# V of the second and third batch by row loads into the odd key spans, instead of by casts and moves, in a fused window attention and shrink MLP

## Chip, cores and metric

One core of one Trainium2 chip. The metric is device time in microseconds of one launch, as the median of the runs; a profiled execution of the same kernel gives the trace. Engines are named as in the profile: PE is TensorE, DVE is VectorE, ACT is ScalarE, POOL is GpSimd, SP is the engine that only issues DMAs. PEld is TensorE's weight load. L12 is line 12 of the kernel.

## What is computed

Attention over 8 batches, 8 heads, 576 tokens and a head of 64, in which a query sees itself and the 63 keys before it; then a two-layer map over the 4608 tokens with 512 features, 2048 wide inside, whose nonlinearity is h - tanh(h).

```python
rel = pos[:, None] - pos[None, :]
scores = np.where((rel >= 0) & (rel < 64), q @ k.T / 8, -1e9)      # per batch and head
attn = softmax(scores)
x = (attn @ v) with the heads side by side                          # 4608 x 512
h = x @ w_in
out = (h - np.tanh(h)) @ w_out
```

## The kernel before, in words

**Tiles of attention.** Heads are worked in pairs (pr, pr + 4); g = 4 b + pr numbers the 32 pairs. The 576 queries of a batch are 9 windows of 64 (NJ = 9). Window j needs the keys of window j - 1 and its own: key span j, 128 keys. `vw[b % 2]` (L71) holds V of a batch as `[128, 9, 8 heads, 65]`: column j is key span j, partitions 0 to 63 the keys of window j - 1 ("lower half"), 64 to 127 those of window j ("upper half"); the 65th value is 1.0, so that the product with V also gives the row sums. Each window's keys thus stand twice: in the upper half of span j and in the lower half of span j + 1. There are two such buffers, so batch b + 2 overwrites batch b.

**The steps of a pair**, by the letters of the plan: q, r, Q, K load Q and K (L87, L99), a and b cast and rearrange them (L111), E and F transpose them on TensorE and move the result out of PSUM (`tr`, L243), R computes scores and their exp (L256), M masks (L266; for b < 2 the mask is added by a matmul, L263, instead), P multiplies with V (`pv`, L270) and divides (`norm`, L277), X or Y turn the outputs into xT, the left operand of the MLP (L288 by TensorE for b < 2, L301 by DMA transposes on SP from b = 2 on). P of one pair uses three PSUM banks that P of the next needs, so norm of a pair stands between them.

**The MLP** runs in 9 chunks of 512 tokens. A half-step h is the unit of the written-out order (loop at L492): an even h holds `hp_mm` (four L317 matmuls of 512 columns, then tanh on ACT, L321, and the subtraction gT on DVE, L327); an odd one holds `yp_mm` (four L337 matmuls) for a group 16 steps earlier. hp uses two PSUM banks in turn, so the L317 group of half-step h needs gT of h - 4 done. Chunk c starts at half-step 32 c. The attention of later batches is laid between half-steps.

**What sets the order.** Nothing is scheduled by a tool: each engine takes its instructions in the order in which they are written (`manual_schedule`). `PLAN` (L419) gives the steps of batches 0 to 2 by half-step, -1 being all that comes before the first L317 matmul; the loop at L451 does so for batches 3 to 7 by formulas. POOL's order matters most: it casts, and it issues all casting DMAs in its one queue. `pace` (L106) makes POOL wait for a gT before it issues K or Q of batches 4 to 7.

**V, three ways.**
- Batch 0: four loads of a pair each (`load_v`, v0x), casts into `vb` (`cast_v`, d0x), nine moves of 65 KB by DMA from `vb` into the upper halves (`keys_v`, L160, k0x; issued by SP, POOL or ACT as the last letter says) and two copies on DVE from upper to lower halves (`shift_v`, z0v). `vb` holds eight tokens in each of 72 partitions.
- Batches 1 and 2: one load of 576 KB (`load_v_all`, L150, steps V1 and V2), four casts on POOL (d1x, d2x), nine moves (k1x, k2x), and the shift: on DVE for batch 1 (z1v), by one DMA on SP of 520 KB for batch 2 (z2s, half-step 31, L170).
- Batches 3 to 7: `load_rows` (L172), five loads with tokens in partitions straight from DRAM, cast by the DMA, into both halves of the odd spans and the upper half of span 8; then `cross_rows` (L178), two DVE copies of 64 partitions that fill the even spans from the odd ones. In this form heads stand in their own order, and `pv` takes heads pr and pr + 4 with a stride (`pr::NP`), where the other form has the pair side by side. The loads stand at half-steps s - 59 to s - 55 and the copies at s - 42, with s about 32 b (L454).

Of the kernel before, what the change touches and what calls it, by code (L numbers as in the profile page):

```python
# [8 lines left out]
BF16 = mybir.dt.bfloat16  # L9
# [6 lines left out]
def kernel(  # L16
# [9 lines left out]
    nc = tc.nc  # L26
    B, H, S, D = q.shape
    NP = H // 2
    NJ = S // 64
    E, P = 6, S // 6  # L30
    EV, PV = 8, S // 8
    NF = S // 128
# [14 lines left out]
    v_pool = ctx.enter_context(tc.tile_pool(name="v", bufs=1))  # L47
# [23 lines left out]
    vw = [const.tile([128, NJ, H, D + 1], BF16, name=f"vw{i}") for i in range(2)]  # L71
# [7 lines left out]
    stage, rows, whole = {}, {}, {}  # L79
# [19 lines left out]
    def load_all(b, n):  # L99

        t = all_pool.tile([P, H, E * D], BF16, tag=n, name=n + "all")
        nc.gpsimd.dma_start(out=t, in_=(q if n == "q" else k)[b].rearrange("h (p e) d -> p h (e d)", e=E))
        for pr in range(NP):
            stage[b * NP + pr, n] = t[:, pr::NP]
# [42 lines left out]
        nc.gpsimd.dma_start(out=t, in_=v[b, pr::NP].rearrange("h (p e) d -> p h (e d)", e=EV))  # L147
        stage[b, pr, "v"] = t

    def load_v_all(b):  # L150
        t = v_pool.tile([PV, H, EV * D], BF16, tag="v", name="vall")
        nc.gpsimd.dma_start(out=t, in_=v[b].rearrange("h (p e) d -> p h (e d)", e=EV))
        for pr in range(NP):
            stage[b, pr, "v"] = t[:, pr::NP]

    def cast_v(b, pr, eng=nc.gpsimd):
        move(eng, vb[:, :, 2 * pr:2 * pr + 2, 0:D].rearrange("p e h d -> p h e d"),
             stage.pop((b, pr, "v")).rearrange("p h (e d) -> p h e d", d=D))
# [3 lines left out]
        eng.dma_start(out=vw[b % 2][64:128, j].rearrange("p h c -> p (h c)"),  # L162
                      in_=vb[8 * j:8 * j + 8].rearrange("p e h c -> p e (h c)"))

    def shift_v(b, j0, j1, eng=nc.sync):
        lo, hi = vw[b % 2][0:64, j0 + 1:j1 + 1], vw[b % 2][64:128, j0:j1]
        if eng is nc.vector:
            eng.tensor_copy(lo, hi)
        else:
            eng.dma_start(out=lo.rearrange("p j h c -> p (j h c)"), in_=hi.rearrange("p j h c -> p (j h c)"))  # L170

    def load_rows(b, i):  # L172

        w, n = vw[b % 2], min(128, S - 128 * i)
        nc.gpsimd.dma_start(out=w[:, 2 * i + 1, :, 0:D] if i < NF else w[64:128, 2 * i, :, 0:D],  # L175
                            in_=v[b, :, 128 * i:128 * i + n].rearrange("h p d -> p h d"))

    def cross_rows(b):  # L178

        w = vw[b % 2]  # L180
        nc.vector.tensor_copy(w[0:64, 2::2], w[64:128, 1::2])
        nc.vector.tensor_copy(w[64:128, 0:NJ - 1:2], w[0:64, 1::2])
# [26 lines left out]
    def more_constants():  # L209
        nc.vector.memset(qT[1], 0.0)  # L210
        nc.vector.memset(kT[1][:, 0:64], 0.0)
        for i in range(2):
            nc.vector.memset(vw[i][0:64, 0], 0.0)

        for h in range(2):
            nc.gpsimd.memset(hide[:, h], 0.0)
            nc.gpsimd.affine_select(hide[:, h], hide[:, h], compare_op=ALU.is_ge, fill=-(2.0 ** 30),
                                    base=-1, pattern=[[-1, 64]], channel_multiplier=1)  # L220
            nc.gpsimd.affine_select(hide[:, h], hide[:, h], compare_op=ALU.is_ge, fill=-(2.0 ** 30),
                                    base=64, pattern=[[1, 64]], channel_multiplier=-1)
# [47 lines left out]
    def pv(g, grp):  # L270
        b, pr = divmod(g, NP)
        for i in range(3):
            j = 3 * grp + i
            nc.tensor.matmul(ps[:, 5 + grp, 130 * i:130 * i + 130], PT[g % NPT][:, j, :],  # L274
                             vw[b % 2][:, j, pr::NP, :] if b > 2 else vw[b % 2][:, j, 2 * pr:2 * pr + 2, :], start=True, stop=True)

    def norm(g):  # L277
        b, pr = divmod(g, NP)
# [71 lines left out]
    def at(h, *fn):  # L350
        items.setdefault(h, []).append(fn)
# [14 lines left out]
    def play(script):  # L366
        for step in script.split():
            what = step[0]
            n = [int(i, 36) for i in step[1:] if i not in "apvs"]
            eng = [ENG[i] for i in step[1:] if i in "apvs"]  # L370
            if what in "qr":
                load(*n, "q" if what == "q" else "k", *eng)
            elif what in "QK":
                load_all(*n, what.lower())
            elif what == "V":
                load_v_all(*n)
            elif what == "a":
                cast(*n, "q", *eng)
            elif what == "b":
                cast(*n, "k", *eng)  # L380
            elif what == "v":
                load_v(*n)
            elif what == "d":
                cast_v(*n, *eng)
            elif what == "k":
                keys_v(*n, *eng)
            elif what == "z":
                for j in (0, 4) if eng[0] is nc.vector else (0,):
                    shift_v(*n, j, j + 4 if eng[0] is nc.vector else NJ - 1, *eng)
            elif what == "E":  # L390
                tr(*n, "q", 3, *eng)
            elif what == "F":
                tr(*n, "k", 2 if n[0] < 2 * NP else 3, *eng)
            elif what == "R":
                scores(*n, (4, 0, 1)[n[1]] if n[0] < NP else 4)
            elif what == "P":
                for i in range(3):
                    pv(*n, i)
                norm(*n)
            elif what == "M":  # L400
                masking(*n)
            elif what == "X":
                b, half, part = n
                x_tr(b, half, 4 * part, 4 + 5 * part, 2 if part == 1 and b < 2 else 3, *eng)
            elif what == "Y":
                x_dma(*n)
            elif what == "w":
                load_w_in(*n)
            elif what == "o":
                load_w_out(*n)  # L410
            elif what == "i":
                make_ident()
            elif what == "n":
                make_mask()
            elif what == "m":
                more_constants()
# [3 lines left out]
        -1: """  # L420
            r2a q0s v02 v03 v00 v01 a0v r0s d00a d01v d02a m i r1p q3p q1a d03p b0a k01s a1v
            k08s k00s b1p k03p n k02s F0a E0av R01 R02 q2p E1av k07p V1 k06a a3p k04p b2v K1 a2a
            R00 F1v k05s r3a E2aa F2a Q1 w0 R10 z0v d12p R22 d13p R12 P0 R11 E3aa R20 P1 d10p
            b3a d11p k12s k13p R21 k16p a7p w1 F3a b4a P2 a4p R30 R31 X000v Q2 R32 P3 b7a X001a
            k10s K2 b5p a6p F4a k18s w2 X010v k11s k17s b6p a5p b9p V2 k15a X011v E4vv""",
        0: "b8p",
        10: "R42 F5v k14s E5aa",
        12: "a8v R41 o2 o1 a9p d20p z1v",
        15: "R50 o3 R40 E6av F6v d21p R51 R52 E7aa P4 d22p R62 F7a R61 bAa o0 d23p P5 k25s R60",
        16: "E8aa k23p aAp R70",  # L430
        20: "R72 k20s X100v k27s X101a P6",
        23: "F8a R71 F9a k21p k22p aBp R80 P7 E9av k26s bBp k24p R82",
        24: "R81 X111v k28s X110a R91",
        31: "R90 z2s EAav M8",
        32: "R92",
        35: "FAa",
        36: "RA1 M9",
# [13 lines left out]
    for g in range(3 * NP, B * NP):  # L451
        b, pr = divmod(g, NP)
        a = 8 * g - 48 - (0, 2, 4)[min(b - 3, 2)]
        s = 32 * b - (0, 2, 4)[min(b - 3, 2)]  # L454
        if b < 7:
            at(a - 7, cast, g, "q")
            at(a, tr, g, "q", 3, nc.scalar, nc.vector)
        else:
            at(a - 14, cast_q, g)
            at(a - 12, bounce, g, "q")  # L460
            at(a - 6, tr_dma, g, "q")
        if b < 7:
            at(a - 5, cast, g, "k")
            at(a + 2, tr, g, "k", 3, nc.scalar)
        else:
            at(a - 13, cast, g, "k")
            at(a - 11, bounce, g, "k")
            at(a - 5, tr_dma, g, "k")
        for i in range(3):
            at(a + 5 + 2 * i, scores, g, i, 4)  # L470
        at(a + 11, masking, g)
        for i in range(3):
            at(a + 13 + i, pv, g, i)
        at(a + 15, norm, g)
        if pr == NP - 1:
            at(a + 16, x_dma, b)
        if pr == 0:
            for i in range(NF + 1):
                at(s - 59 + i, load_rows, b, i)
            at(s - 42, cross_rows, b)  # L480
        if pr == 0:
            if b < 4:
                at(s - 64, load_all, b, "q")
                at(s - 63, load_all, b, "k")
            else:
                hq, hk = s - (60 if b < 7 else 68), s - (64 if b < 7 else 72)
                for h, f in (hq, (load_all, b, "q")), (hk, (load_all, b, "k")):
                    at(h, pace, h)
                    at(h, *f)

    LAG = 16
    for h in range(min(items), 2 * (16 * NC + LAG) + 2):  # L492
        n = h // 2
        c, m = divmod(n, M)
# [41 lines left out]
```

## Time and profile before

| what | value |
|---|---|
| runs | 353.31, 349.85 and 349.43 us |
| median | 349.85 us |
| profiled execution | 354.17 us, its span 352.4 us, 5650 instructions |
| busy in the span | PE 314.9, DVE 205.0, ACT 192.8, POOL 107.9 us |
| L317 and L337 matmuls (512 columns) | 148.0 and 140.3 us |
| DMA | 38.31 MB in 70315 packets, 47104 of them under 512 B |
| loads of rows of V (L175), 25 | issue 0.86 us of POOL, landing 3.8 / 7.3 / 15.9 us after issue (min, median, max) |
| loads of V, 576 KB (L152), 2 | issue 0.85 us of POOL, landing 11.50 and 9.40 us after issue |
| casts of V on POOL (L85) | 1.06 us each |
| DVE copies of 64 x 2080 (L168, L181, L182) | 0.70 us each |

A page of the profile gives the busy time of each engine, then 40 equal slices of the span (8.8 us each) with busy tenths, the clock that was granted to TensorE, and the DMA engines. The chain of waits goes back from the last instruction, at each step to what released it. A timeline row reads: start, duration, engine, line, operation, output and input, form, count, and in brackets the idle time before it with what ended it. A row of the windows has, for each of PE, PEld, DVE, ACT and POOL, the busy time and the number of instructions, then the mean granted clock, the DMA share and the rate in GB/s.

### The profile page before, as it was taken

What the parts mean: (1) busy time and instruction counts of PE and PEld (TensorE: products, weight loads), DVE (VectorE), ACT (ScalarE), POOL (GpSimd) and SP (SyncE); (2) the same over time, 40 slices, a digit from 0 to 9 for tenths busy, and PEclk for the clock granted to TensorE, in tenths of its full rate; (3) what the DMA queues carried; (4) which work ended last, traced back from release to release, by engine and by line L of the source; (5) the groups of instructions that cost most, each with busy time, mean ns of one, the idle gap of its engine ahead of it and who ended that gap; (6) DMA issues with size and microseconds to landing.
All of it is one profiled execution on the core that took longest, in us unless ns stands there. A gap on an engine that the chain in (4) does not pass through costs nothing.

```text
span 352.4 us, 5650 instructions
## 1 busy us (share of the span) xinstructions
PE 314.9 (89%) x2142; PEld 180.1 (51%) x2173; DVE 205.0 (58%) x324; ACT 192.8 (55%) x347; POOL 107.9 (31%) x156
## 2 busy tenths in 40 slices
PE   0277778897899999999999999999999999999995
PEld 0266456554555555555555555555555444444442
DVE  1335776863777668766867686676666433333300
ACT  1466578863565666566666666655554444444421
POOL 7728623953203760265034342810000000000000
PEclk9999999998999999999999999999999999999999
DMA  8699999999204990893099469986601400010012
GB/s 172 122 160 186 162 190 173 172 145 180 38 32 74 165 91 34 158 156 46 30 163 156 72 79 198 140 198 132 175 32 38 119 32 30 30 61 30 30 71 80
DMA packets 70315, 38.31 MB, mean 109 GB/s; under 512 B 47104, under 2 KB 64448, under 8 KB 70224
## 3 DMA queue, kind: packets, MB, share of 16 engines
q0 software_dynamic: 40032, 18.22, 46.4%
q1 hardware_dynamic: 29488, 18.71, 20.1%
q10 hardware_dynamic: 768, 1.02, 1.0%
q8 instruction: 17, 0.28, 0.3%
q14 instruction: 10, 0.08, 0.1%
HBM read 36.70 MB, written 11.21 MB: 136 GB/s over the span
## 4 chain that ended last, share of the span: by engine, by line
PE 69%; DMA 15%; POOL 6%; DVE 4%; issue 3%; ACT 2%; ACTq 0%; POOLq 0%; SPq 0%; DVEq 0%
PE ps L337 32%; PE ps L317 28%; DMA vall<-in_v_dram 5%; DMA vw<-vb 4%; DMA kall<-in_k_dram 4%; PE ps L274 4%; PE ps L260 3%; DMA vw<-vw 3%; PE ps L247 2%; POOL vb L85 2%; DVE xs L285 1%; POOL vw L162 1%; DVE gT L327 1%; POOL qb L85 1%; ACT th L321 1%
## 5 line engine op out<-in xcount | busy, mean ns | idle before, releaser
L327 DVE TENSOR_TENSOR gT<-ps,th 128x512 bf16<-128x512 f32 x144 | 99.2, 691 | 87.4 <-ACT th L321 84.2
L317 PE MATMUL ps<-xT,wi 128*128 128x512 bf16 x576 | 148.0, 381 | 1.8 <-DVE gT L327 1.7
L337 PE MATMUL ps<-w_out_sb,gT 128*128 128x512 bf16 x545 | 140.3, 379 | 1.8 <-ACT ysb L342 0.2
L321 ACT ACTIVATE th<-ps 128x512 f32<-128x512 f32 x144 | 85.9, 597 | 80.3 <-PE ps L317 80.1
L317 PEld LDWEIGHTS <-wi 128*128 128x128 bf16 x576 | 61.1, 113 | 47.8 <-issue 3.6
L337 PEld LDWEIGHTS <-gT 128*128 128x128 bf16 x576 | 54.0, 97 | 56.1 <-issue 0.9
L264 ACT ACTIVATE pt<-ps 128x384 bf16<-128x384 f32 x96 | 46.9, 489 | 45.0 <-PE ps L260 37.5
L285 DVE TENSOR_TENSOR xs<-ps,rc 64x576 bf16<-64x576 f32 x64 | 48.3, 755 | 1.5
L260 PE MATMUL ps<-qt,kt 128*128 128x128 bf16 x288 | 36.9, 228 | 6.3 <-ACT pt L264 3.8
L274 PE MATMUL ps<-vw,pt 128*128 128x130 bf16 x288 | 30.3, 228 | 6.1 <-DMA vw<-vw 2.3
L274 PEld LDWEIGHTS <-pt 128*128 128x128 bf16 x288 | 23.0, 101 | 22.5 <-issue 3.2
L342 ACT ACTIVATE ysb<-ps 128x512 f32<-128x512 f32 x36 | 21.5, 596 | 16.0 <-PE ps L337 16.0
L260 PEld LDWEIGHTS <-kt 128*128 128x128 bf16 x288 | 24.6, 102 | 9.8 <-ACT kt L83 1.9
L85 DVE COPY qt<-ps 64x576 bf16<-64x576 bf16 x24 | 18.2, 758 | 17.3 <-ACT qt L83 17.2
L85 POOL COPY qb<-qall 96x768 bf16<-96x768 bf16 x24 | 20.0, 833 | 20.6 <-DMA qall<-in_q_dram 18.3
L85 POOL COPY kb<-kall 96x768 bf16<-96x768 bf16 x26 | 21.6, 833 | 12.2 <-DMA kall<-in_k_dram 11.9
L83 ACT ACTIVATE qt<-ps 64x576 bf16<-64x576 bf16 x32 | 20.4, 636 | 1.4 <-PE ps L247 1.2
L175 POOL DMA_DIRECT2D vw<-in_v_dram x25 | 21.1, 860 | 0.0
L109 POOL COPY tick<-gT 1x1 bf16<-1x1 bf16 x8 | 1.4, 180 | 62.9 <-DVE gT L327 55.3
L83 ACT ACTIVATE kt<-ps 128x576 bf16<-128x576 bf16 x25 | 16.2, 648 | 4.3 <-PE ps L247 4.2
L268 DVE TENSOR_TENSOR pt<-pt,ps 128x1152 bf16<-128x1152 bf16 x24 | 17.9, 744 | 0.0
L247 PE MATMUL ps<-ident,kb 96*128 96x96 bf16 x168 | 12.8, 217 | 2.0 <-ACT xT L83 0.9
(55 smaller groups left out, 144.9 us busy)
## 6 DMA issues: line engine op xcount, KB each, us to landing
out_dram<-ysb SPq DMA_DIRECT2D x36, 256.0 KB
kall<-in_k_dram POOLq DMA_DIRECT2D x7, 576.0 KB, 6.8
qall<-in_q_dram POOLq DMA_DIRECT2D x7, 576.0 KB, 9.1
vw<-in_v_dram POOLq DMA_DIRECT2D x20, 128.0 KB, 8.3
w_out_sb<-in_moe_w_out_dram POOLq DMA_DIRECT2D x4, 512.0 KB, 8.6
vall<-in_v_dram POOLq DMA_DIRECT2D x2, 576.0 KB, 10.4
qd<-qz SPq DMA_DIRECT2D x4, 288.0 KB
vw<-vb SPq DMA_DIRECT2D x16, 65.0 KB
```

Source lines behind the costliest of these rows:

```text
L83: nc.scalar.activation(o, i, ACT.Copy)
L85: eng.tensor_copy(o, i)
L175: nc.gpsimd.dma_start(out=w[:, 2 * i + 1, :, 0:D] if i < NF else w[64:128, 2 * i, :, 0:D], in_=v[b, :, 128 * i:128 * i + n].rearrange("h p ...
L260: nc.tensor.matmul(sp[:, i, :], kT[g % NR][:, 64 * j:64 * j + 128], qT[g % NR][:, :, 64 * j:64 * j + 64], start=True, stop=g >= 2 * NP)
L264: nc.scalar.activation(PT[g % NPT][:, 3 * grp:3 * grp + 3, :], sp, ACT.Exp, scale=scale)
L274: nc.tensor.matmul(ps[:, 5 + grp, 130 * i:130 * i + 130], PT[g % NPT][:, j, :], vw[b % 2][:, j, pr::NP, :] if b > 2 else vw[b % 2][:, j, 2 ...
L285: nc.vector.tensor_tensor(xo[r, :, :, pr, :], ov[r, :, :, h, 0:D], rc[r].to_broadcast([64, 3, 3, 64]), ALU.mult)
L317: nc.tensor.matmul(hp, w_in_tile(ki, m), chunk_tile(c)[:, :, ki % 2, 64 * (ki // 2):64 * (ki // 2) + 64], start=(ki == 0), stop=(ki == 3))
L321: nc.scalar.activation(th, hp, ACT.Tanh)
L327: nc.vector.tensor_tensor(gT[c][:, m, :], hp, th, ALU.subtract)
L337: nc.tensor.matmul(yp, gT[c][:, m, s * 128:(s + 1) * 128], w_out_sb[:, m, :], start=(m == 0), stop=(m == M - 1))
L342: nc.scalar.activation(ysb, ps[:, yp_bank(c, s), :], ACT.Copy)
```

## The change

Batches 1 and 2 take the way of batches 3 to 7: V1 and V2 become five `load_rows` each at the same places of the plan, their casts and moves (d1x, d2x, k1x, k2x) fall away, z1 and z2 become `cross_rows` on DVE at the places of the former shifts (half-steps 12 and 31), and `pv` takes the strided heads from batch 1 on. `vw[1]` gets its ones by a memset on DVE, since no move from `vb` brings them; `vw[0]` keeps those of batch 0. And for batches 3 to 7 the row loads come nine half-steps sooner (s - 68), which for batch 3 is ahead of its loads of Q and K, and for batch 4 is half-step 58, where the transposes of xT for batch 2 stand (Y2).

```diff
-    def load_v_all(b):
-        t = v_pool.tile([PV, H, EV * D], BF16, tag="v", name="vall")
-        nc.gpsimd.dma_start(out=t, in_=v[b].rearrange("h (p e) d -> p h (e d)", e=EV))
...
-    def shift_v(b, j0, j1, eng=nc.sync):
...
+    def shift_v(b, j0, j1):
+        nc.vector.tensor_copy(vw[b % 2][0:64, j0 + 1:j1 + 1], vw[b % 2][64:128, j0:j1])
...
         for i in range(2):
+            if i == 1:
+                nc.vector.memset(vw[i][:, :, :, D], 1.0)
             nc.vector.memset(vw[i][0:64, 0], 0.0)
...
-                             vw[b % 2][:, j, pr::NP, :] if b > 2 else vw[b % 2][:, j, 2 * pr:2 * pr + 2, :], start=True, stop=True)
+                             vw[b % 2][:, j, pr::NP, :] if b > 0 else vw[b % 2][:, j, 2 * pr:2 * pr + 2, :], start=True, stop=True)
...
             elif what == "V":
-                load_v_all(*n)
+                for i in range(NF + 1):
+                    load_rows(*n, i)
...
             elif what == "z":
-                for j in (0, 4) if eng[0] is nc.vector else (0,):
-                    shift_v(*n, j, j + 4 if eng[0] is nc.vector else NJ - 1, *eng)
+                if n[0] > 0:
+                    cross_rows(*n)
+                for j in (0, 4) if n[0] == 0 else ():
+                    shift_v(*n, j, j + 4)
...
-            R00 F1v k05s r3a E2aa F2a Q1 w0 R10 z0v d12p R22 d13p R12 P0 R11 E3aa R20 P1 d10p
-            b3a d11p k12s k13p R21 k16p a7p w1 F3a b4a P2 a4p R30 R31 X000v Q2 R32 P3 b7a X001a
-            k10s K2 b5p a6p F4a k18s w2 X010v k11s k17s b6p a5p b9p V2 k15a X011v E4vv""",
+            R00 F1v k05s r3a E2aa F2a Q1 w0 R10 z0v R22 R12 P0 R11 E3aa R20 P1
+            b3a R21 a7p w1 F3a b4a P2 a4p R30 R31 X000v Q2 R32 P3 b7a X001a
+            K2 b5p a6p F4a w2 X010v b6p a5p b9p V2 X011v E4vv""",
...
-        10: "R42 F5v k14s E5aa",
-        12: "a8v R41 o2 o1 a9p d20p z1v",
-        15: "R50 o3 R40 E6av F6v d21p R51 R52 E7aa P4 d22p R62 F7a R61 bAa o0 d23p P5 k25s R60",
-        16: "E8aa k23p aAp R70",
-        20: "R72 k20s X100v k27s X101a P6",
-        23: "F8a R71 F9a k21p k22p aBp R80 P7 E9av k26s bBp k24p R82",
-        24: "R81 X111v k28s X110a R91",
-        31: "R90 z2s EAav M8",
+        10: "R42 F5v E5aa",
+        12: "a8v R41 o2 o1 a9p z1",
+        15: "R50 o3 R40 E6av F6v R51 R52 E7aa P4 R62 F7a R61 bAa o0 P5 R60",
+        16: "E8aa aAp R70",
+        20: "R72 X100v X101a P6",
+        23: "F8a R71 F9a aBp R80 P7 E9av bBp R82",
+        24: "R81 X111v X110a R91",
+        31: "R90 z2 EAav M8",
...
-                at(s - 59 + i, load_rows, b, i)
+                at(s - 68 + i, load_rows, b, i)
```

More of the change, by code (lines that the diff above doesn't have):

```diff
@@ L148, in load_v @@
         stage[b, pr, "v"] = t
-    def load_v_all(b):
-        t = v_pool.tile([PV, H, EV * D], BF16, tag="v", name="vall")
-        nc.gpsimd.dma_start(out=t, in_=v[b].rearrange("h (p e) d -> p h (e d)", e=EV))
-        for pr in range(NP):
-            stage[b, pr, "v"] = t[:, pr::NP]
     def cast_v(b, pr, eng=nc.gpsimd):
@@ L163, in keys_v @@
                       in_=vb[8 * j:8 * j + 8].rearrange("p e h c -> p e (h c)"))
-    def shift_v(b, j0, j1, eng=nc.sync):
[L166 to L170, printed above, removed]
+    def shift_v(b, j0, j1):
+        nc.vector.tensor_copy(vw[b % 2][0:64, j0 + 1:j1 + 1], vw[b % 2][64:128, j0:j1])
     def load_rows(b, i):
```

## The prediction, made before the changed kernel ran

> **What bounds the kernel now.** I read the page's slices first, for the stage that is not yet bound by TensorE; then the chain of waits, for what that stage waits for; then TensorE's and GpSimd's timelines around the places that the chain names.
>
> The slices (40 of 8.8 us each, busy tenths and granted clock):
>
> ```profile
> PE   0277778897899999999999999999999999999995
> PEclk9999999998999999999999999999999999999999
> ```
>
> From slice 11 on (88 us) TensorE is at 9 tenths to the end. A change to V can win only ahead of that, in about 88 us, and whatever it wins there moves the whole rest forward. Two things stick out: low tenths in slices 1 to 5, and slice 10 (79 to 88 us), the only one with a clock below 9.
>
> The chain that ended last names the cause of both (start, us, what):
>
> ```profile
> 16.82 10.27 DMA vw<-vb
> 27.29 4.49 POOL vb L85 x4
> ...
> 36.39 13.66 DMA kall<-in_k_dram
> 50.97 9.40 DMA vall<-in_v_dram
> 61.94 2.04 POOL vb L85 x2
> ...
> 69.83 4.09 DMA vw<-vb
> 74.11 9.84 DMA vw<-vw
> 83.99 1.05 PE ps L274 x8
> ```
>
> The end hangs on V of the third batch (b = 2): load, casts in POOL, moves by DMA into the upper halves, the shift by DMA (L170, 9.84 us), and only then pv of P9. TensorE's timeline and two windows give the price:
>
> ```profile
> 81.46 0.22 PE L274 MATMUL ps<-vw,pt 128*128 128x130 bf16 x1
> 83.99 1.05 PE L274 MATMUL ps<-vw,pt 128*128 128x130 bf16 x8 [2.32 <-DMA vw<-vw]
> ...
> 88.10 1.02 PE L317 MATMUL ps<-xT,wi 128*128 128x512 bf16 x4
> ```
>
> ```profile
> 80.00:90.00 10.00, 7.63 (x45) 4.33 (x45) 3.71 (x7) 3.45 (x6) 3.83 (x5) 0.83 2.02 142
> 90.00:100.00 10.00, 8.99 (x77) 5.52 (x76) 7.98 (x13) 5.90 (x12) 1.59 (x2) 1.00 0.07 28
> ```
>
> 2.32 us of standstill, and after it a mean granted clock of 0.83 over 10 us (third number from the end): 1.7 us of clock missing, that is 3.4 us at half rate. The work from 83.99 to 88.10 (8 pv, 3 scores, 6 transposes, 8 matmuls of 512) takes 2.6 us at the spacing of the stretch behind it (0.057, 0.057, 0.043 and 0.215 each); it took 4.11. So the half rate cost 1.5, and the whole place 3.8.
>
> The other place is P0, the first pv of the kernel, and what GpSimd does just ahead of it:
>
> ```profile
> 25.83 0.64 PE L274 MATMUL ps<-vw,pt 128*128 128x130 bf16 x4
> 27.13 0.27 PE L274 MATMUL ps<-vw,pt 128*128 128x130 bf16 x1 [0.66 <-DMA vw<-vb]
> 27.92 0.59 PE L274 MATMUL ps<-vw,pt 128*128 128x130 bf16 x4 [0.52 <-DVE vw L168]
> ```
>
> ```profile
> 15.21 0.84 POOL L152 DMA_DIRECT2D vall<-in_v_dram  x1
> 16.05 0.83 POOL L85 COPY qb<-qall 96x768 bf16<-96x768 bf16 x1
> 16.82 0.58 POOL L162 DMA_DIRECT2D vw<-vb  x1
> ```
>
> **The change part by part.**
>
> *V of b = 2 (V2, z2).* Gone: the load at 50.97, four casts (61.94 and 64.44 in the chain are three of them), nine key moves and the 9.84 us shift. In their place five row loads and two VectorE copies at half-step 31. The loads are issued from 50.97 on; a group of five took 4.20 us of POOL (220.38), and row loads land 3.8 / 7.3 / 15.9 us after issue (min, median, max, L175). Last issue 54.5, landed by 58.3 to 70.4. The copies stand at about 73.3 in VectorE's order, P9 at 81.5. So at the slowest landing of the trace P9 no longer waits: minus 2.32, minus 1.5 of clock.
>
> For the clock a page and a row differ. Row: a 2.32 us gap and then 0.83. The Trainium skill, TensorE: Matmul & The Clock Gate, section Why this matters for your kernels, asks only that gaps of over about 3 us be avoided. By that rule this gap would have left the clock alone and the 1.5 would not be there to win; the trace says it was lost in this execution. Another execution may place its gap differently, which I use below.
>
> *The copies z2 on VectorE.* Two of 0.70 us, as L181 and L182 show. VectorE's order at half-step 31 becomes: gT of half-step 30 (ends 73.27), the copies, a qT move (0.76), a masking (0.76), gT of half-step 32. That last one now ends at 74.95 + 0.69 + 1.2 = 76.84 instead of 75.64, and the L317 group at 76.06 needs its bank: a stall of 0.8. Bounds: 0 (TensorE idle elsewhere) to 1.4 (both copies). The nearest row, the same copies of b = 3 at 101.29 followed by gT and a masking, left TensorE idle 0.49 at 104.12. I take 0.8.
>
> *V of b = 1 (V1, z1).* Gone: load, four casts (27.29, 4.49 us), nine moves. VectorE's two shift copies become two cross copies (1.31 to 1.40 us): nothing, they stand at 48.85 and P4 at 53.63. One memset more on VectorE, about 0.1 like vb's 0.11 at 1.76, at 11 us where VectorE then waits 0.60 for a load: nothing. On POOL the casts go, but they stood after the loads K1, Q1 and w0; the next cast waits for Q1's landing anyway, so the 4.49 are worth little. If Q1 landed sooner they would come out as earlier issues of w1, Q2 and K2; I count none.
>
> What V1 costs: five issues (4.20) in place of one (0.84), ahead of the cast at 16.05, key move 4 of batch 0 (16.82), K1, Q1 and w0. All move back by 3.36. The order of the changed kernel also lets each GpSimd DMA wait for the eighth before it: w0 now waits for the first row load, which by the same 3.8 to 7.3 lands at 19.0 to 22.5, while w0's turn comes at 22.3. K1, Q1 and w0 were issued at 17.39 to 18.95 and are fetched one after the other; K1's is first read by a cast at 33.40 and w0 at 39.63, so the cover is over 10 us. Key move 4 is the one with a reader: the second shift of batch 0 and P0. It is issued at 15.21 + 4.20 + 0.83 = 20.2. Before, it took 10.27 because V's 576 KB stood ahead of it. Alone a move or row load lands in 3.8: 24.0. At the median of the row loads, 7.3: 27.5, against 27.09 before. Middle 25.8, which lets the shift (0.70) end at 26.5 instead of 27.87 and takes both waits of P0 (0.66 + 0.52) out: minus 1.2. Bounds: minus 1.6 (the norm after P0 could start at 27.0 for 28.55) to plus 3.4 (10.27 again). P0, its norm and P1 to P3 follow each other without slack up to the first L317 at 39.63, so the amount passes on.
>
> The rule that speaks against this part: the Trainium skill, DMA: Bandwidth & Descriptors, Specifications, wants 512 B a transfer and says that smaller ones are done as read-modify-write. Rows of 64 bf16 are 128 B. The page gives no time for it; were the loads to take twice as long as the trace's, key move 4 would land at 27.8 to 34.8 and the sum below would be between minus 0.2 and plus 6.8. The 25 row loads in this trace are such packets already, so I go by theirs.
>
> *Later V nine half-steps sooner.* Row loads of b = 3 are issued before Q3 and K3 instead of behind them; they wait for P7 (64.79 in TensorE's timeline), so POOL reaches Q3 about at 69.5 instead of 70.38, since it no longer casts or moves V2 there. Q3 is read by POOL at 83.16, 10 us before its transposes (93.35): covered. Row loads of b = 4 now come at half-step 58, after PB (104.12), together with the SP transposes xT at 106.65 (3.20 us for both). These feed the L317 group at 112.78. Slack after issue is 2.9 us; the rows can take engines for up to 4.2. Price 0 (before, no L317 waits for a DMA on xT) to 1.3. The nearest row, no such wait anywhere, is the lower end, and I take 0. The first load of b = 4 waits on POOL for PB; behind it stands a cast of K for b = 3 that ran before 92.7 and now runs after 105, its transposes stand at 115.90: covered, and without the cover TensorE would wait for them. The key moves and the shift leave SP and the DMA engines: 18 moves of 65 KB and one of 520 KB less, counted at nothing because no other wait on a DMA is left between 40 and 81 us but 0.2 for wi.
>
> **Sum.** Minus 2.32, minus 1.5, minus 1.2, plus 0.8: minus 4.2. The profiled execution took 354.17 us (span 352.4 and 1.8 around it), so it would take 350.0. But its own time is 4.3 above the median of 349.85, and from 88 us on TensorE runs without a break. So those 4.3 must mostly come out of the first 88 us, and the waits on DMAs are the likeliest to be shorter there; the run of 353.31 stands 3.9 above that of 349.43, about the 3.8 of P9. I let half of the 4.3 be the place of P9: of 3.8 about 1.7 is left to win in the median. Minus 1.7, minus 1.2, plus 0.8: minus 2.1, 347.7.
>
> **The rivals.**
> - *The whole gain (0.25).* The runs shown have the wait and the half clock as the profile does, and are shorter by something else. For it: a chain of 47 us through V2. Against it: the 4.3. Minus 4.2: 345.6.
> - *Hidden anyway (0.20).* Without the profiler the shift ends in time. P9 gains nothing, P0 0 to 0.9, z2 costs 0.8: 349.8 to 350.7.
> - *V1 blocks batch 0 (0.08), the slower one.* Row loads at the front of POOL hold key move 4 up. The worst landing of a row load, 15.9, would put it at 36.1, P0 9.0 us late, and with minus 1.7 and plus 0.8 the time at 358.0; it decides against the change when the move lands after 28.0 (27.09 plus the 0.9 left), and by over 1% after 31.5. Against it: those 15.9 had 1.1 MB of Q3 and K3 ahead of them.
> - *xT late at half-step 64 (0.05).* Rows of b = 4 beside the transposes: plus 1.3, 349.0.
>
> **How the numbers follow.** Forecast 0.42, own range 346.4 to 349.2. Together with the whole gain and the hidden case the range is 345.0 to 351.0: about 0.1 is left out on either side. A measurement of this kernel tells about 1% (3.5 us) from no change: below 346.35 is faster, above 353.35 slower. Faster: the whole gain and a part of the forecast, 0.30. Slower: 0.08. The rest, 0.62, is within.
>
> **What would show it.** Right: no DMA wait ahead of P9, granted clock 1.00 in the window 80 to 90, the first L317 group near 38.4, a new wait of TensorE on gT near 76. Wrong: pv of P0 waiting for vw later than 28; a wait on xT at half-step 64; or the wait at P9 gone in the trace and the median unchanged, which would mean that only the profiled execution had it.

## The result, and the profile after

| | before | after |
|---|---|---|
| median of 20 runs each | 351.05 us (349.43 to 353.75) | 353.24 us (351.77 to 356.19) |
| ratio, with its 95% interval | | 1.0061 [1.0041, 1.0081] |
| profiled execution (span) | 354.17 us (352.4) | 354.56 us (352.8) |

The kernel became 0.6% slower, some 2.2 us. The forecast was 347.7 us, and the range ended at 351.0. Ratios, and counts of executions further down, leave out runs that are more than 1.5% above the fastest run of the same kernel. Lines move: before's L274 (pv) is L266 after, L317 is L309, L337 is L329, L175 (a row load) is L165, L162 (a key move) is L156, L168 (the shift) is L160.

The two profiled executions end 0.4 us apart, but not because nothing happened between. From the two TensorE timelines, the start of the first L317 (before) or L309 (after) product of a half-step, in us:

| half-step | before | after | after minus before | what lies just ahead |
|---|---|---|---|---|
| 0 | 39.6 | 40.6 | +1.0 | P0 to P3 |
| 2 | 40.6 | 42.3 | +1.7 | half clock |
| 34 | 74.1 | 75.8 | +1.7 | |
| 36 | 76.1 | 78.7 | +2.6 | the copies z2 |
| 42 | 85.6 | 85.0 | -0.7 | P9 |
| 44 | 88.1 | 86.7 | -1.4 | half clock in before |
| 62 | 110.5 | 109.2 | -1.4 | |
| 64 | 112.8 | 113.0 | +0.2 | xT of batch 2 |

From half-step 66 on the difference stays at 0.1 us to TensorE's last group; the rest of the 0.4 comes behind it. So four places move, three of them the wrong way: P0 and its clock +1.7, z2 +0.9, P9 -4.0, xT +1.5.

The slices of after, to be laid beside those of before:

```profile
PE   0276788889898999999999999999999999999995
PEclk9999899999999999999999999999999999999999
```

The low clock of slice 10 has gone and stands in slice 5 (35 to 44 us) instead. The windows of after place it (busy time and count for PE, PEld, DVE, ACT, POOL; then the granted clock, the DMA share, GB/s):

```profile
35.60:39.00 3.40, 1.63 (x25) 1.24 (x22) 3.00 (x6) 2.45 (x6) 3.40 (x5) 1.00 1.04 157
39.00:42.40 3.40, 3.35 (x20) 2.08 (x21) 2.46 (x5) 0.47 (x1) 1.90 (x3) 0.50 1.20 170
```

```profile
80.00:90.00 10.00, 9.95 (x74) 5.80 (x74) 6.02 (x10) 5.48 (x11) 2.70 (x4) 1.00 0.10 30
```

A granted clock of 0.50 for 3.4 us, right where the MLP starts; 1.00 at P9's place, with TensorE busy for 9.95 of 10 us.

The chain of waits no longer goes through V2, but through the key move of batch 0 behind V1's row loads, and then through z2:

```profile
15.18 4.23 POOL vw L165 x5
19.40 0.71 POOL qb L85
20.12 7.56 DMA vw<-vb
27.76 0.71 DVE vw L160
28.51 0.61 PE ps L266 x4
...
75.02 0.70 DVE vw L171
75.73 0.70 DVE vw L172
76.46 0.76 DVE qt L85
77.25 0.76 DVE pt L260
78.01 0.61 DVE gT L319
```

TensorE's timeline of after at the four places:

```profile
27.72 0.27 PE L266 MATMUL ps<-vw,pt 128*128 128x130 bf16 x1 [1.28 <-DMA vw<-vb]
28.51 0.59 PE L266 MATMUL ps<-vw,pt 128*128 128x130 bf16 x4 [0.52 <-DVE vw L160]
...
78.66 1.02 PE L309 MATMUL ps<-xT,wi 128*128 128x512 bf16 x4 [0.72 <-DVE gT L319]
...
84.00 0.69 PE L266 MATMUL ps<-vw,pt 128*128 128x130 bf16 x9
...
112.95 1.05 PE L309 MATMUL ps<-xT,wi 128*128 128x512 bf16 x4 [1.39 <-DMA xT<-xs]
```

Before had no bracket at half-steps 36 and 64:

```profile
76.06 1.03 PE L317 MATMUL ps<-xT,wi 128*128 128x512 bf16 x4
...
112.78 1.03 PE L317 MATMUL ps<-xT,wi 128*128 128x512 bf16 x4
```

P0 waits longer for the same move (1.28 for 0.66). Half-step 36 waits for gT. P9's nine products run without a bracket: the wait of 2.32 is gone. And half-step 64 waits for xT. The issue queues behind that last one: GpSimd's in after, then SP's in after, then SP's in before:

```profile
103.32 0.89 POOL L165 DMA_DIRECT2D vw<-in_v_dram  x1 [12.84 <-PE ps L266]
...
104.96 3.32 POOL L165 DMA_DIRECT2D vw<-in_v_dram  x4
```

```profile
105.27 4.10 SPq L298 DMA_TRANSPOSE xT<-xs  x2
```

```profile
106.65 3.20 SPq L306 DMA_TRANSPOSE xT<-xs  x2
```

The rows of b = 4 leave within the same 5 us as the two transposes, whose issue takes 4.10 us for 3.20 before.

### The profile page after: what moved, and what is told of

It reads as the page before. It is cut to its first block, busy times and chain, and to the rows that moved or that the text cites. A ratio compares the mean times of both kernels' runs of the same rounds, so it can differ in the third digit from the quotient of the medians.

```text
span 352.8 us, 5616 instructions
## 1 busy us (share of the span) xinstructions
PE 314.5 (89%) x2142; PEld 180.0 (51%) x2173; DVE 207.5 (59%) x327; ACT 192.9 (55%) x347; POOL 103.9 (29%) x150
## 4 chain that ended last, share of the span: by engine, by line
PE 75%; DVE 8%; DMA 6%; ACT 4%; issue 3%; POOL 3%; ACTq 0%; DVEq 0%; POOLq 0%
PE ps L329 32%; PE ps L309 31%; PE ps L266 5%; PE ps L252 4%; DVE xs L277 3%; PE ps L239 2%; DMA xT<-xs 2%; DMA vw<-vb 2%; DMA vall<-in_v_dram 2%; DVE gT L319 2%; ACT th L313 2%; POOL vw L165 1%; ACT pt L256 1%; ACT qt L83 1%; DVE qt L85 1%
## 5 line engine op out<-in xcount | busy, mean ns | idle before, releaser
L309 PE MATMUL ps<-xT,wi 128*128 128x512 bf16 x576 | 148.1, 381 | 3.8 <-DVE gT L319 2.4
L329 PE MATMUL ps<-w_out_sb,gT 128*128 128x512 bf16 x545 | 140.2, 379 | 1.8 <-ACT ysb L334 0.2
L309 PEld LDWEIGHTS <-wi 128*128 128x128 bf16 x576 | 61.1, 113 | 50.4 <-issue 4.8
L329 PEld LDWEIGHTS <-gT 128*128 128x128 bf16 x576 | 53.9, 97 | 55.8 <-issue 0.5
L165 POOL DMA_DIRECT2D vw<-in_v_dram x35 | 30.0, 874 | 32.3 <-PE ps L252 17.9
L266 PE MATMUL ps<-vw,pt 128*128 128x130 bf16 x288 | 29.8, 225 | 4.5 <-DVE pt L260 1.3
L266 PEld LDWEIGHTS <-pt 128*128 128x128 bf16 x288 | 22.8, 100 | 20.6 <-issue 3.9
L239 PE MATMUL ps<-ident,qb 96*128 96x96 bf16 x168 | 13.0, 219 | 1.1 <-ACT qb L83 1.1
```

The source lines that it names most:

```text
L239: nc.tensor.transpose(tp[:, e, :], src[:, e, :], ident[:P, :P])
L309: nc.tensor.matmul(hp, w_in_tile(ki, m), chunk_tile(c)[:, :, ki % 2, 64 * (ki // 2):64 * (ki // 2) + 64], start=(ki == 0), stop=(ki == 3))
L329: nc.tensor.matmul(yp, gT[c][:, m, s * 128:(s + 1) * 128], w_out_sb[:, m, :], start=(m == 0), stop=(m == M - 1))
```

## Experiments

Theory after the result: V1's rows in front of key move 4 cost time at P0 (A), z2 on DVE costs about 1 us (B), rows of b = 4 beside the xT transposes cost 1 to 2 us (C), and P9 wins less than these together. Rivals: that P9's gain is smaller than the trace shows; that all later V coming sooner, not b = 4 alone, does the harm; that the wait at P0 is that of any load ahead of move 4, in before as well. Kernels of one group ran on one chip and share the runs of before; the ratio is to these, with its 95% interval.

**Group 1 (before 352.12 us, 35 runs): parts of the change.**

e1 is after with the later V where it was:

```diff
-                at(s - 68 + i, load_rows, b, i)
+                at(s - 59 + i, load_rows, b, i)
```

> The changed kernel with the later V back at s - 59; V1 and V2 still by rows. Theory: three costs outweigh the removed wait at P9: V1's row loads ahead of key move 4 (about 0.6 to 1.7 us), the copies z2 on VectorE (0.9) and the transposes xT that wait beside the row loads of b = 4 (1.4). Then this kernel is 1.4 us faster than the changed one, ratio to before about 1.002, and no L309 matmul waits for xT at half-step 64. Rival: the loss is all in V1 and z2, the wait on xT belongs to the profiled execution alone: ratio stays at 1.006.

Measured: 352.08 us, 1.000 [0.9971, 1.0029]. Moving later V back is worth 0.6% against the 1.0061 of after, and 0.3% against 1.0034, its second measurement (h1 below); which batch does it, this run cannot say.

e2 puts back only b = 4:

```diff
-                at(s - 68 + i, load_rows, b, i)
+                at(s - (59 if b == 4 else 68) + i, load_rows, b, i)
```

> The changed kernel with the row loads of b = 4 alone back at s - 59, those of b = 3 and 5 to 7 still nine half-steps sooner. Theory: only b = 4 collides with transposes that are due within 6 half-steps, so this equals the kernel with all of them back (ratio about 1.002) and has no wait on xT. Rival: the earlier loads of b = 3, ahead of its Q and K, cost too: then it is slower than the kernel with all of them back.

Measured: 352.32 us, 0.998 [0.9947, 1.0013]. Putting b = 4 alone back does as well as putting all of them back: the others' place costs nothing that shows.

e3 is before with V of b = 1 alone by rows (part of the edit; the ones, the strided heads and z1 change as in after):

```diff
-                load_v_all(*n)
+                if n[0] == 1:
+                    for i in range(NF + 1):
+                        load_rows(*n, i)
+                else:
+                    load_v_all(*n)
...
-            R00 F1v k05s r3a E2aa F2a Q1 w0 R10 z0v d12p R22 d13p R12 P0 R11 E3aa R20 P1 d10p
+            R00 F1v k05s r3a E2aa F2a Q1 w0 R10 z0v R22 R12 P0 R11 E3aa R20 P1
```

> The kernel before with V of b = 1 alone by rows (V1, z1); V2 with casts, moves and the shift by DMA, later V at s - 59. Theory: P0 is later by 0.6 and the first L317 group by about 1, and the wait at P9 gets shorter by the same or more, since V2's chain starts from K2 and not from TensorE: ratio 1.000 to 1.004. Rival: V1 carries the whole loss: 1.006 or more.

Measured: 353.53 us, 1.0025 [0.9994, 1.0056]. Its trace held a surprise. TensorE at P9 in e3, with V2 still loaded, cast, moved and shifted by DMA:

```profile
80.97 1.03 PE L339 MATMUL ps<-w_out_sb,gT 128*128 128x512 bf16 x4
81.83 0.76 PE L276 MATMUL ps<-vw,pt 128*128 128x130 bf16 x9
82.43 0.33 PE L262 MATMUL ps<-qt,kt 128*128 128x128 bf16 x3
```

No wait. With V1's casts and moves gone, V2's old chain arrived in time in this execution. And still the kernel is not faster, so V1 by rows takes away elsewhere what it gives at P9.

e4 is before with V of b = 2 alone by rows (the same edit for `n[0] == 2`, with z2 as two DVE copies).

> The kernel before with V of b = 2 alone by rows (V2, z2); V1 and the later V as before. Theory: the wait at P9 and its half clock are in the unprofiled runs only in part, z2 costs 0.9: ratio 0.993 to 1.000 and no wait at P9. Rival (the whole gain is in all runs): minus 3.0 us, ratio 0.9915. Rival (nothing of it is in the unprofiled runs): 1.0025.

Measured: 350.79 us, 0.9959 [0.9927, 0.9991]. P9 without a wait, and B in its trace (TensorE):

```profile
76.00 1.02 PE L317 MATMUL ps<-xT,wi 128*128 128x512 bf16 x4 [0.97 <-DVE gT L327]
...
81.34 0.69 PE L274 MATMUL ps<-vw,pt 128*128 128x130 bf16 x9
```

So V2's part wins 1.4 us net (0.0041 of 352.1). With the copies at about 1.0 (the wait here, and h4 below), P9 itself is worth about 2.4 in the runs: an estimate from these two, each of which carries over 1 us of uncertainty.

**Group 2 (before 351.52 us, 22 runs): mend A and B, and C alone.**

f1 is e1 with z2 moved to GpSimd at half-step 20:

```diff
-        20: "R72 X100v X101a P6",
+        20: "R72 X100v X101a P6 z2p",
...
-        31: "R90 z2 EAav M8",
+        31: "R90 EAav M8",
```

> The changed kernel with all later V back at s - 59 (which measured 1.000 of before) and the two copies z2 on GpSimd at half-step 20, when GpSimd waits, instead of on VectorE at 31. Theory: the wait of an L309 matmul on gT near half-step 36 (0.72 to 0.79 in the traces) goes: minus 0.8 us, ratio 0.998, and no wait over 0.3 there. Rival: GpSimd's own casts behind the copies come late, or its copies slow VectorE's beside them: ratio 1.000 or above.

Measured: 351.37 us, 0.9999 [0.9976, 1.0022], against 1.000 of e1 in the other group: no gain. The gT wait is gone from its trace, but P0's wait is 1.51 there, and its profiled execution fell back to half clock from 23 to 36.7 us. By the medians this is inconclusive on B (more on the clock below).

f2 is e1 with V1's rows behind key move 4 (the key moves are k07p, k06a and k04p, the last of them move 4):

```diff
-            k08s k00s b1p k03p n k02s F0a E0av R01 R02 q2p E1av k07p V1 k06a a3p k04p b2v K1 a2a
+            k08s k00s b1p k03p n k02s F0a E0av R01 R02 q2p E1av k07p k06a a3p k04p V1 b2v K1 a2a
```

> The changed kernel with all later V back at s - 59 and V1's five row loads issued after key move 4 of batch 0 instead of ahead of it. Theory: key move 4 lands near 20 us, pv of P0 no longer waits for a DMA (0 to 1.88 us in four traces with V1 by rows, mean about 0.9), though it may wait for the shift on VectorE: minus 0.5 to 1.5 us, ratio 0.996 to 0.9985. Rival: what is late is not the order on GpSimd but the ACT queue's key move 6 and Q/K loads beside the small packets: P0 still waits, ratio 1.000.

Measured: 349.64 us, 0.9961 [0.9941, 0.9981]. GpSimd's order and TensorE's P0 in f2:

```profile
15.29 0.59 POOL L156 DMA_DIRECT2D vw<-vb  x1
15.87 4.26 POOL L165 DMA_DIRECT2D vw<-in_v_dram  x5
```

```profile
25.13 1.18 PE L266 MATMUL ps<-vw,pt 128*128 128x130 bf16 x9
```

The move lands at 19.23, 3.9 us after issue, and P0 runs in one piece of nine. A holds; its size comes from h3 and f3.

f3 is e1 with both edits.

> Both edits at once: key move 4 ahead of V1, z2 on GpSimd at half-step 20, later V at s - 59. Theory: the sum, minus 1.3 to 2.3 us, ratio 0.9935 to 0.9965 of before. Rival: as for the two by themselves; 1.000.

Measured: 348.53 us, 0.9924 [0.9902, 0.9947]. On the same chip that is 0.4% under f2, from which it differs by z2 alone, and 0.75% under f1, from which it differs by the place of V1 alone. In its trace the two copies take 1.92 us each on GpSimd (0.70 on DVE), and TensorE is not idle from 70 to 80 us:

```profile
57.88 1.92 POOL L171 COPY vw<-vw 64x2080 bf16<-64x2080 bf16 x1 [0.61 <-DMA vw<-in_v_dram]
59.86 1.92 POOL L172 COPY vw<-vw 64x2080 bf16<-64x2080 bf16 x1
```

```profile
70.00:80.00 10.00, 10.00 (x69) 5.42 (x67) 5.98 (x9) 6.38 (x12) 3.83 (x5) 1.00 1.76 131
```

f4 is before with only the rows of b = 4 sooner:

```diff
-                at(s - 59 + i, load_rows, b, i)
+                at(s - (68 if b == 4 else 59) + i, load_rows, b, i)
```

> The kernel before with one edit: the row loads of b = 4 at s - 68. Theory: the transposes xT of batch 2 share the DMA engines with these loads and the L317 group of half-step 64 waits for them 1 to 2 us, all else equal: ratio 1.003 to 1.006 and a wait on DMA xT in the trace. Rival: the wait needs the rest of the change (TensorE ahead by the wait at P9 that is gone): in the kernel before TensorE arrives later, no wait on xT, ratio 1.000.

Measured: 354.97 us, 1.0099 [1.0069, 1.0129], the clearest single loss of the study, 3.5 us. TensorE at half-step 64 in f4:

```profile
111.61 0.33 PE L260 MATMUL ps<-qt,kt 128*128 128x128 bf16 x3
113.94 1.06 PE L317 MATMUL ps<-xT,wi 128*128 128x512 bf16 x4 [2.01 <-DMA xT<-xs]
```

C holds, without any V1 or V2. The wait shows 2.0 of the 3.5; the other 1.5 were not found.

**Group 3 (before 351.51 us, 22 runs): is move 4 the whole of A, and how far may b = 4 go?**

g1 is before with the order of f2: V1's one load of 576 KB behind move 4.

> The kernel before with one edit: V1 (still one load of 576 KB) is issued after key move 4 of batch 0 instead of ahead of it. Theory: whatever V load stands ahead of key move 4 in GpSimd's queue delays P0, small packets or large; so P0's wait on a DMA goes here too: minus 0.5 to 1.5 us, ratio 0.996 to 0.9985. Rival: only the small packets of the row loads disturb batch 0, the large load does not: ratio 1.000.

Measured: 352.31 us, 1.0016 [0.9982, 1.0050]: no gain. Move 4 landed at 19.69, but the second shift (L168 on DVE) still waited:

```profile
21.66 0.70 DVE L168 COPY vw<-vw 64x2080 bf16<-64x2080 bf16 x1
26.98 0.70 DVE L168 COPY vw<-vw 64x2080 bf16<-64x2080 bf16 x1 [4.63 <-DMA vw<-vb]
```

The shift reads several moves. With move 4 out of the way it was, by the order of issue and landing, the one that ACT issues at 18.87 (k06a), now beside the big load. So the order pays with rows and not with the big load: my account of P0 by move 4 alone fell for before, and holds for after only. It was the big load that held move 4 itself in before: 10.27 us from issue to landing there, 3.79 in g1.

g2 is f3 with later V sooner for b = 3, 5, 6 and 7 but not for b = 4; that is after with all three places mended. The edit of the later V, against after:

```diff
-                at(s - 59 + i, load_rows, b, i)
+                at(s - (59 if b == 4 else 68) + i, load_rows, b, i)
```

> The kernel with both edits (0.9924 of before) and the later V of b = 3 and 5 to 7 at s - 68 again, b = 4 at s - 59. Theory: no transposes within reach, nothing to win or lose: ratio 0.990 to 0.995, no wait on xT. Rival: the loads of b = 3 ahead of Q and K, or of b = 5 to 7 beside their transposes, cost 1 us or more: 0.996 or above.

Measured: 348.23 us, 0.9898 [0.9860, 0.9936]. The best kernel of the study; from f3 it is not told apart.

g3 and g4 are f3 with two, or all five, of the row loads of b = 4 sooner (`68 if b == 4 and i < 2 else 59`, and `68 if b == 4 else 59`).

> The kernel with both edits and two of the five row loads of b = 4 at s - 68, the rest at s - 59: a smaller dose of the packets beside the transposes xT. Theory: the wait on xT grows with the packets that share the DMA engines with the transposes: 0 to 0.7 us for two loads against 1.4 to 2.0 for five. Rival: one load is enough, since transposes queue behind whatever is there: 1.4 or more.

> The kernel with both edits and all five row loads of b = 4 at s - 68. Theory: the wait on xT of 1.4 to 2.0 us appears, and with what it does to the clock the time rises by 1.4 to 3.5 us: ratio 0.9965 to 1.0025. Rival: TensorE is about 5 us earlier here, GpSimd's loads too, so they meet as before but with more slack: under 1 us.

Measured: g3 348.38 us, 0.9900 [0.9866, 0.9934], no xT wait; g4 349.29 us, 0.9923 [0.9894, 0.9951], with this on TensorE:

```profile
109.50 1.05 PE L309 MATMUL ps<-xT,wi 128*128 128x512 bf16 x4 [1.14 <-DMA xT<-xs]
```

The wait is there with five loads and not with two. In time the three kernels lie too close together to be told apart.

**Group 4 (before 352.31 us, 35 runs): from after, one place mended at a time.**

> The changed kernel once more, as the yardstick of this call: 1.006 of before.

> The changed kernel with the row loads of b = 4 alone back at s - 59, beside the changed kernel on the same chip. Theory: 1.4 to 2.0 us of wait on xT go: 0.4 to 0.6% below the yardstick. Rival (price 3 us or more, as the kernel with this edit alone measured, 1.0099): 0.8% or more below it.

> The changed kernel with V1 issued after key move 4 as its only edit. Theory: the wait of P0 on a DMA goes, and the half clock near the first L309 group more often than not: 1 to 1.7 us, 0.3 to 0.5% below the yardstick. Rival: TensorE that comes earlier only waits longer for xT: 0.1% or less.

> The changed kernel with z2 on GpSimd at half-step 20 as its only edit. Theory: the wait on gT near half-step 36 (0.7 to 1.0 in the traces) goes: 0.2 to 0.3% below the yardstick. Rival: the copies on GpSimd delay what stands behind them, or TensorE waits longer for xT: no difference.

| kernel | edit on after | median | ratio | less than h1 |
|---|---|---|---|---|
| h1 | none | 353.45 us | 1.0034 [1.0000, 1.0067] | |
| h2 | as e2 | 352.16 us | 0.9990 [0.9958, 1.0023] | 0.44% |
| h3 | as f2 | 350.59 us | 0.9963 [0.9933, 0.9993] | 0.71% |
| h4 | as f1 | 352.51 us | 1.0006 [0.9974, 1.0038] | 0.28% |

Each difference carries about 0.47% of uncertainty (the two half-widths added in squares), so only h3's stands by itself. C is carried by f4, B by f3 against f2, and A also by f3 against f1. The sum is a check: h1 less the three is +0.34 - 1.43 = -1.09%, and g2, with all three, measured -1.02%.

How the waits varied from trace to trace matters for the sizes:

| wait of TensorE | traces |
|---|---|
| P0 for a key move, V1's rows ahead of move 4 | after 1.28, e1 0, e2 1.88, e3 0.50, f1 1.51, h1 0.21, h2 0.87, h4 0.63 |
| the same, the 576 KB load ahead of it | before 0.66, e4 0, f4 0.50 |
| the same, rows behind it (f2, h3, f3, g2, g3, g4) | 0 in all |
| half-step 64 for xT, b = 4 sooner by five loads | after 1.39, f4 2.01, g4 1.14, h1 0.33, h3 0.42, h4 0 |
| half-step 36 for gT, z2 on DVE | after 0.72, e1 0.79, e2 0.72, e4 0.97, f2 0.97, h1, h2 and h3 0.72 |

DMA waits spread from 0 to 1.9 or 2 us, the wait on an engine's order hardly at all. Move 4, with the rows ahead, landed at 25.65 to 28.11, 6.2 to 8.2 us after issue; with the 576 KB load ahead, at 25.79 to 27.09 (8.9 to 10.3 after issue); ahead of both, at 19.2 to 20.0 (3.8 to 4.2 after issue).

A part of the rest of the spread goes with the granted clock. Each execution has its mean; an execution at 1.00 but for 3.4 us at half rate has about 0.995. Sorted by it:

| kernels | executions below 0.997 | median of those at 0.997 or above |
|---|---|---|
| before, groups 1 to 4 | 70 of 106 | 350.2 to 351.0 us by group (36) |
| V1's rows ahead of move 4: after, e1, e2, e3, f1, h1, h2, h4 | 68 of 103 | after 352.57 (7), e1 351.53 (3), e2 351.73 (5), e3 351.01 (2), h1 351.57 (4), h2 350.97 (6), f1 350.39 (4), h4 351.27 (4) |
| V1's rows behind move 4: f2, f3, g2, g3, g4, h3 | 16 of 52 | f2 349.52 (6), h3 350.38 (11), f3 348.30 (4), g2 348.14 (4), g3 348.33 (5), g4 349.27 (6) |

Two readings. Between h1 and h3 1.2 us of the 2.5 to 2.9 remain among executions at 0.997 or above, and the other half goes with fewer executions below it (1 of 12 in h3, 8 of 12 in h1). And f1 against e1 differ by 1.1 us there, B's size; but these are four runs against three, of two groups.

This mean leaves out the start of the kernel. The windows give a clock of 1.00 there, yet the same nine products of P1 take 1.14 us in after and 0.67 in f2:

```profile
30.97 1.14 PE L266 MATMUL ps<-vw,pt 128*128 128x130 bf16 x9
```

```profile
28.18 0.67 PE L266 MATMUL ps<-vw,pt 128*128 128x130 bf16 x9 [0.18 <-DVE xs L277]
```

In after, products of 128 columns follow each other every 0.107 us up to 32.1 us and every 0.055 from there on: TensorE starts at half rate. In f2 the step comes at 27.8. So the place of P0 is best priced whole, from its first product to the first product of the MLP; the last column has the time at which the starting half rate ended:

| V1 | traces | first product of P0 to first of the MLP | half rate ended at |
|---|---|---|---|
| rows ahead of move 4 | after, e1, e2, e3, f1, h1, h2, h4 | 13.6 to 16.3 us, mean 14.6 | 30.8 to 38.3 us |
| 576 KB load ahead of it | before, e4, f4 | 12.2 to 13.8 us, mean 13.2 | 29.1 to 32.5 us |
| rows behind it | f2, f3, g2, g3, g4, h3 | 11.8 to 12.1 us, mean 11.9 | 26.9 to 29.2 us |

(e1, f1 and g2 had 3.4 us of full rate at about 20 us and lost it again. g1, the big load behind the move, took 15.2 and ended its half rate at 36.6.) By these traces rows ahead of the move cost 1.4 us against the big load, and 2.7 against rows behind it, the longer half rate within them.

## Why the prediction was wrong, step by step

**P9: right in the trace, wrong in what it was put down to.** Minus 2.32 and minus 1.5 were forecast and -4.0 came. But the step gave all of it to V2's new way. In e3's trace V1's part alone ended the wait: the prediction said of POOL's freed time "the 4.49 are worth little". It had looked for worth at K and Q, not at V2's own chain.

**The halving for the median: a weak argument, an acceptable number.** "Its own time is 4.3 above the median of 349.85" rested on three runs. The median of 20 runs is 351.05. Runs of before in the groups reach 354.79, so the profiled 354.17 is no case apart. The step took 1.7 for P9; the runs give about 2.4 (e4 and z2's 1.0). This made the forecast gain smaller, so it is not what failed.

**z2 on DVE: right.** 0.8 was forecast; the wait on gT is 0.72 to 0.97, h4 gives 1.0 (0.28%, within its uncertainty), and f3 against f2 1.3 (0.37%).

**V1: the step that failed, with the wrong sign.** "Alone a move or row load lands in 3.8: 24.0. At the median of the row loads, 7.3: 27.5. [...] Middle 25.8", hence "minus 1.2". The move landed at 27.68, 7.56 after issue, and the first group of the MLP, named for 38.4, came at 40.61. The 7.3 was the row that described this move, standing behind row loads in one queue; the 3.8 described one with nothing ahead, which h3 shows (19.42, 3.8 after issue). The middle of two unlike cases described neither. The 7.3 also mixed two sizes: 8.3 at the median of the 20 loads of 128 KB, 4.1 for the five of 64 KB. In the runs, rows ahead of move 4 cost about 2.5 us against rows behind it (h3 0.71%, f3 against f1 0.75%; f2 against e1, of two groups, 0.39%). Taking after as +1.2 (h1), -2.4 for P9, +1.0 for z2 and +1.55 for xT leaves +1.05 for V1: an estimate, where -1.2 stood, and a rough one, since each of its terms carries over 1 us. Two things beside it agree: e3, which changes V1 alone, measured +0.9 us (-0.2 to +2.0, the gain at P9 included), and the traces give +1.4 up to the first product of the MLP. The -1.2 was to be had, with the move first: 1.05 - 2.5 is -1.45.

A part of the 2.5 is the clock, a term that the prediction had for P9 only. The starting half rate ends later with the rows ahead, as the table above shows; that it does so because P0 waits is not shown by itself. Then there are the falls after it. In after's profile the clock was half from 39.0 to 42.4, with no gap of TensorE over 0.85 us in the 8 us ahead; before's profile shows the same gaps in the same order and 1.00. What differs is where they fall: within a trace the changes of clock lie whole multiples of 3.41 us apart, and the stretch of that length ahead of 39.0 had TensorE busy for 1.63 of 3.40 us in after, while the one in before (35.9 to 39.3) had 2.12. Over all 18 traces, nine of the ten full-rate stretches with TensorE busy for less than half of it were followed by half rate, four of the 21 with 0.56 to 0.63, and none with more: a count over these traces. Over all executions such falls are as common with V1's rows ahead (68 of 103) as in before (70 of 106) and rarer with the move ahead (16 of 52). So V1 did not make them more frequent; they show less often where P0 does not wait, which is a count and not a proof of the cause. The Trainium skill, TensorE: Matmul & The Clock Gate, section Why this matters for your kernels, asks that gaps over about 3 us be avoided. Here a gap of 2.32 (before) and a stretch of short ones (35.6 to 39.0, TensorE busy 1.63 of 3.40 us) were each followed by 3.4 us at half rate, so in this kernel the rule is too mild.

**xT: the second failing step.** "Price 0 [...] to 1.3. The nearest row, no such wait anywhere, is the lower end, and I take 0." The wait in the trace was 1.39; h2, f4, and g4 against g2 give 1.55 (0.44%, within its uncertainty), 3.5 and about 1 us. "No such wait anywhere" was true of a kernel in which no row load stood beside a transpose of xT: a row without the neighbour that the change adds. Before's trace had a sign of the price: one pair of these transposes took 5.87 us to issue, just behind the 576 KB load of K that left at 205.39, though TensorE did not wait there.

```profile
206.48 5.87 SPq L306 DMA_TRANSPOSE xT<-xs  x2
```

The prediction had the slack (2.9 us) and the engines' share (up to 4.2) right, and the second is larger than the first. The Trainium skill, DMA: Bandwidth & Descriptors, section Issuing engines are not separate DMA queues, says that DMAs of all issuers run on the same 16 engines and interleave; the issue of the transposes, 4.10 us for 3.20, agrees, though they leave from SP and the rows from GpSimd.

**Nothing for the other parts: right.** Q3 and K3 later, fewer moves, the memset, later V of b = 3, 5, 6 and 7 (g2 is as fast as f3): no wait answers to them.

**The rivals.** Both slower ways came, at 0.08 and 0.05, and together, V1's in a small form: the move landed at 27.68, short of the 28.0 from which that rival was to decide. They had been priced one at a time, each against an otherwise successful change. From the forecast's own terms, V1 at 0 and xT at +1.3 in place of -1.2 and 0 make +0.4 of -2.1: the sign hung on two choices between bounds, both taken on the cheap side, and the chances did not show that. The rival that P9's gain is hidden anyway did not come: e4's median still gained 1.4 us from V2's part.

**Open.** What the rest of f4's 3.5 us is; which of the stretches between 0.56 and 0.63 fall to half rate; and why ACT's move holds P0 up beside the big load (g1) but not beside rows (f2).

## What to carry to other kernels

Before a load is put ahead of a small transfer that somebody waits for, put the transfer first: here the place of one word of the plan was worth 0.4 to 0.75%. A row of the trace prices a DMA only with the same neighbours in front of it; where the change brings new ones, take the dear bound as the likely one if the neighbours' time exceeds the slack. And when several hidden costs each hang on slack, price them together, since one edit can use up all of them at once.

## What the chip showed that was not expected

- A move of 65 KB landed 6.2 to 8.2 us after issue behind five row loads of 128 B packets, 8.9 to 10.3 behind one load of 576 KB, and 3.8 to 4.2 ahead of both.
- DMA transposes on SP next to row loads of GpSimd: two issues took 4.0 to 4.2 us for 3.2, and their reader waited 0 to 2.0 us, differently in each execution.
- The granted clock fell to 0.50 for 3.4 us after a stretch with no gap over 0.85 us, and in before after one of 2.32. What the stretches ahead share is TensorE busy for less than half of 3.4 us (1.63 and 1.38).
- At the start TensorE ran at half rate up to 26.9 to 38.3 us, by the spacing of its products, while the windows gave a clock of 1.00.
- The copy of 64 x 2080 bf16 to other partitions took 1.92 us on GpSimd and 0.70 on DVE. It still paid there (f3 against f2), since GpSimd had the time and DVE's order did not.
